# One recurrence unit moved from TensorE transposes to the DMA crossbar, two running sums to a subtraction, one set of decays to small transfers, and all orders written anew

## The chip, the cores and the metric

The kernel runs on one core of one Trainium2 chip. The metric is device time of one execution in microseconds (us); where several executions were timed, their median counts. A core has TensorE (PE, matrix products; its weight loads are listed as PEld), VectorE (DVE), ScalarE (ACT), GpSimd (POOL), and the queue of SyncE (SP), which here only issues DMA transfers. Each engine works its own list of instructions strictly in order and waits on semaphores for the others.

## The reference

Two parts, one behind the other. First a gated linear recurrence for 4 batches of 8 heads over 768 steps with head width 48:

```python
f = 1.0 / (1.0 + np.exp(-f_logit))
for t in range(S):
    state = f[:, :, t, :, None] * state + np.einsum('bhd,bhe->bhde', k[:, :, t], v[:, :, t])
    y[:, :, t] = np.einsum('bhd,bhde->bhe', q[:, :, t], state)
```

Then a gated feed-forward network over the 3072 tokens, with the 8 heads side by side as 384 features and 1536 hidden features:

```python
gate = np.maximum(x @ w_gate, 0.0)
val = x @ w_val
return (gate * val @ w_out)
```

## The kernel before, in words

**Units.** The recurrence is cut into 12 units: `seq` orders them (batch 0 to 3 for the first 256 steps, then for the second, then for the third). A unit is 256 steps of one batch, as two chunks y of 128 steps; a token's even and odd step (index i) lie side by side in one partition of the loaded tile. For each unit `unit(u)` does this:

- Four loads of 384 KB (f, k, q, v) from SP (L449), into four buffers each, so that the load of unit u+4 waits until unit u no longer needs the buffer.
- `exp` and `ln` of the gate on ACT (L536, L538), then running sums along the steps. These are products of TensorE with triangular matrices (L545, L546), two matmuls for the odd steps and, where the unit's setting `even` is `PE`, two more for the even steps. Where `even` is `DVE`, the even ones are the odd ones less one term, a VectorE subtraction in PSUM (L549).
- Exponentials of the sums on ACT (L557, L560, L567) and products with k and q, called hats (L579, L585). With `kps` the exponential for k stays in PSUM and VectorE multiplies; with `qps` the same holds for q.
- k and q must be turned so that features lie in partitions. For units in the set `pe_hats` this is 8 transposes of TensorE for k and 8 for q (L634), each followed by one copy out of PSUM (settings `tk`, `tq`; L647). For the others the hats are written 64 partitions at a time, and two crossbar transposes of the DMA (L655), issued from SP, do it.
- v is copied into a padded tile in pieces of 64 partitions (L619); units in `pe_hats` have two more pieces in another tile (`vrest`, L623).
- Scores of k and q per chunk (L669), masked on VectorE (L683) or copied by ACT and masked on POOL (L678, L680); the state's update (L723 with 8 matmuls of 128 rows, L734 with 16 of 64 rows for `pe_hats`); the output products (L767, L774, L778), whose copies give `xT`, the input of the network, either directly or through one more crossbar transpose (L797).
- The decay of the state over a chunk: a small TensorE sum of 9 matmuls (`total`, L706 and L710) with one ACT exponential (L714), or, where `td` is set and `qps` is not, one store of two rows to DRAM (L690) and four strided loads of them (L699), all from SP.

**The network.** Two units give a group g of 512 tokens. Of its 12 slices of hidden features each takes three matmuls for the gate and three for the value (`ffn_hidden`, L814), ACT's relu (L819) and VectorE's product into `gT` (L821). `ffn_out` takes three matmuls per third of the features and 128 tokens (L837), four such triples give one output tile, which is copied (L851) and stored (L858). Group 0 starts in halves of 256 tokens (r0 and r2) for the first three slices. The weights come in 12 transfers of 288 KB in bf16, four each for `wg`, `wv`, `wo`, three hidden slices each, issued from POOL (L477) because they convert the type.

**Order.** Nothing is ordered by the program text alone: `SEQUENCE` holds, for each engine and for SP, a list of operation numbers written out by hand or by a search, `HOMES` the order in which the tiles of PSUM share the 8 banks, and `FILLERS` a number of matmuls on zeros that TensorE works ahead of a named operation. `Plan.needs` puts the semaphore waits where the order does not already imply them. So an engine with an early wait holds up all that is behind it in its list.

Of the kernel before, what the change touches and what calls it, by code (L numbers as in the profile page):

```python
# [7 lines left out]
F32 = mybir.dt.float32  # L8
BF16 = mybir.dt.bfloat16
# [28 lines left out]
class Plan:  # L38
# [80 lines left out]
    def needs(self, warm):  # L119
# [69 lines left out]
    "ACT": [  # L189
# [9 lines left out]
    "DVE": [  # L199
# [20 lines left out]
}  # L220
HOMES = [
    [
        312, 14, 16, 18, 28, 34, 66, 47, 81, 86, 58, 124, 104, 132, 116, 108, 135, 111, 139, 174, 169, 148, 181, 216, 161, 262, 230, 195, 229, 198,
        232, 211, 236, 269, 251, 246, 258, 288, 297, 301],
    [
        0, 6, 12, 22, 63, 65, 31, 36, 69, 43, 52, 71, 59, 97, 172, 103, 164, 143, 150, 182, 215, 163, 190, 196, 201, 202, 266, 240, 239, 244, 274,
# [23 lines left out]
def bass_hgrn2_outer__then__ffn_reglu_kernel(  # L250
# [14 lines left out]
    HD = H * D  # L265
# [14 lines left out]
    pe_hats = {0, 1, 2, 3, 5}  # L280
# [5 lines left out]
    NU = len(seq)  # L286
# [689 lines left out]
```

## Time and profile before

| what | value |
|---|---|
| median of 3 runs | 194.19 us (193.44 to 194.41) |
| profiled execution | 193.8 us, of which the span from first to last instruction is 192.0 us |
| busy in the span | PE 181.1 us, DVE 126.3, ACT 118.5, POOL 82.8 |
| bytes | 31.89 MB moved, a mean of 166 GB/s |
| granted TensorE clock | 1.00 |

The profile is one execution. A row of a timeline gives the start, the time to the end of the last instruction of the row, engine, line, operation, tiles, form, count, and in brackets the idle time ahead of it with what ended it. Ends of matmuls are modelled, so they overlap; the pace of TensorE is read from one start to the next. In the rows of transfers the last number is the time from issue to landing.

### The profile page before, as it was taken

What the parts mean: (1) busy time and instruction counts of PE and PEld (TensorE: products, weight loads), DVE (VectorE), ACT (ScalarE), POOL (GpSimd) and SP (SyncE); (2) the same over time, 40 slices, a digit from 0 to 9 for tenths busy, and PEclk for the clock granted to TensorE, in tenths of its full rate; (3) what the DMA queues carried; (4) which work ended last, traced back from release to release, by engine and by line L of the source; (5) the groups of instructions that cost most, each with busy time, mean ns of one, the idle gap of its engine ahead of it and who ended that gap; (6) DMA issues with size and microseconds to landing.
All of it is one profiled execution on the core that took longest, in us unless ns stands there. A gap on an engine that the chain in (4) does not pass through costs nothing.

```text
span 192.0 us, 4436 instructions
## 1 busy us (share of the span) xinstructions
PE 181.1 (94%) x1746; PEld 101.0 (53%) x1770; DVE 126.3 (66%) x238; ACT 118.5 (62%) x233; POOL 82.8 (43%) x110
## 2 busy tenths in 40 slices
PE   3998799998999999999999999999999999999994
PEld 1365474545654646455655456454655554445563
DVE  4189864879499999987669989445277452242451
ACT  4998668681997877978687857247702642433511
POOL 4458553994247256754696749007500320000000
DMA  6999999999599999999974792564144050000325
GB/s 156 324 325 285 205 253 206 242 231 199 145 310 220 229 323 255 245 213 189 259 202 79 153 232 59 120 130 123 50 107 79 0 164 3 20 0 0 81 66 164
DMA packets 79088, 31.89 MB, mean 166 GB/s; under 512 B 71254, under 2 KB 79068, under 8 KB 79068
## 3 DMA queue, kind: packets, MB, share of 16 engines
q1 hardware_dynamic: 74268, 28.08, 59.7%
q0 software_dynamic: 4800, 3.54, 11.9%
q8 instruction: 14, 0.23, 0.5%
q14 instruction: 6, 0.05, 0.1%
HBM read 25.96 MB, written 4.73 MB: 160 GB/s over the span
## 4 chain that ended last, share of the span: by engine, by line
PE 75%; DMA 6%; DVE 6%; ACT 4%; SPq 3%; issue 3%; POOL 2%; POOLq 0%
PE ps L814 43%; PE ps L837 22%; DMA wv<-in_moe_w_val_dram 4%; SPq L449 3%; DMA v_in<-in_v_dram 3%; PE ps L669 2%; PE ps L767 2%; DVE gT L821 2%; DVE ptm L683 1%; PE ps L634 1%; ACT ptm L678 1%; ACT relu L819 1%; PE ps L545 1%; DVE vpad L380 1%; POOL vpad L383 1%
## 5 line engine op out<-in xcount | busy, mean ns | idle before, releaser
L821 DVE TENSOR_TENSOR gT<-relu,ps 128x512 bf16<-128x512 bf16 (+1 forms) x75 | 47.7, 660 | 32.9 <-PE ps L814 19.6
L819 ACT ACTIVATE relu<-ps 128x512 bf16<-128x512 f32 (+1 forms) x75 | 41.8, 582 | 37.1 <-PE ps L814 29.1
L837 PE MATMUL ps<-wo,gT 128*128 128x384 bf16 (+2 forms) x300 | 56.2, 320 | 0.9 <-DVE vrest L380 0.8
L814 PE MATMUL ps<-xT,wv 128*128 128x512 bf16 (+1 forms) x214 | 54.6, 370 | 1.3 <-DMA wv<-in_moe_w_val_dram 0.4
L814 PE MATMUL ps<-xT,wg 128*128 128x512 bf16 (+1 forms) x214 | 54.2, 370 | 1.2 <-DMA wg<-in_moe_w_gate_dram 0.5
L680 POOL TENSOR_TENSOR ptm<-ptm,seen 128x512 bf16<-128x512 bf16 x21 | 24.0, 1155 | 39.9 <-ACT ptm L678 39.8
L837 PEld LDWEIGHTS ps<-wo,gT 128*128 128x128 bf16 x300 | 28.0, 98 | 22.4 <-DVE vrest L380 1.2
L814 PEld LDWEIGHTS ps<-xT,wg 128*128 128x128 bf16 x225 | 21.1, 98 | 21.3 <-DMA wg<-in_moe_w_gate_dram 0.8
L814 PEld LDWEIGHTS ps<-xT,wv 128*128 128x128 bf16 x225 | 20.9, 98 | 20.5 <-DVE hats L579 0.6
L683 DVE TENSOR_TENSOR ptm<-ps,seen 128x512 bf16<-128x512 f32 x27 | 18.1, 685 | 1.9 <-PE ps L669 1.7
L585 DVE TENSOR_TENSOR hats<-k_in,ps 64x384 bf16<-64x384 f32 x28 | 15.4, 550 | 5.2 <-ACT ps L567 4.7
L515 POOL TENSOR_TENSOR st<-ssum,dec 128x384 bf16<-128x384 f32 x16 | 13.3, 832 | 11.0 <-DVE ssum L512 10.1
L585 POOL TENSOR_TENSOR hats<-q_in,expo 64x384 bf16<-64x384 f32 x16 | 15.9, 995 | 4.8 <-ACT expo L560 3.8
L678 ACT ACTIVATE ptm<-ps 128x512 bf16<-128x512 f32 x21 | 11.8, 595 | 8.5 <-PE ps L669 8.5
L579 POOL TENSOR_TENSOR hats<-q_in,expo 128x384 bf16<-128x384 f32 x11 | 10.9, 999 | 12.8 <-ACT expo L560 8.2
L382 ACT ACTIVATE osb<-ps 128x384 f32<-128x384 f32 x13 | 6.5, 499 | 12.0 <-PE ps L837 12.0
L560 ACT ACTIVATE expo<-ps 128x384 f32<-128x384 f32 x20 | 9.4, 492 | 3.4 <-DVE ps L549 2.8
L512 DVE TENSOR_TENSOR ssum<-ps,st 128x384 f32<-128x384 f32 x16 | 8.8, 553 | 3.7 <-PE ps L723 2.3
L536 ACT ACTIVATE f_in<-f_in 128x768 f32<-128x768 f32 x12 | 10.2, 847 | 1.1 <-DMA f_in<-in_f_logit_dram 1.0
L567 ACT ACTIVATE ps<-ps 128x384 f32<-128x384 f32 x22 | 10.6, 497 | 0.0
L538 ACT ACTIVATE bneg<-f_in 128x768 bf16<-128x768 f32 x12 | 10.2, 848 | 0.2
L383 DVE COPY osb<-ps 128x384 f32<-128x384 f32 (+2 forms) x12 | 6.2, 520 | 5.5 <-PE ps L837 5.5
(86 smaller groups left out, 185.1 us busy)
## 6 DMA issues: line engine op xcount, KB each, us to landing
f_in<-in_f_logit_dram SPq DMA_DIRECT2D x12, 384.0 KB, 5.8
v_in<-in_v_dram SPq DMA_DIRECT2D x12, 384.0 KB, 5.3
q_in<-in_q_dram SPq DMA_DIRECT2D x12, 384.0 KB, 4.9
k_in<-in_k_dram SPq DMA_DIRECT2D x12, 384.0 KB, 5.4
out_dram<-osb SPq DMA_DIRECT2D x15, 192.0 KB, 2.1
out_dram<-osb SPq DMA_DIRECT2D x16, 96.0 KB, 2.2
wg<-in_moe_w_gate_dram POOLq DMA_DIRECT2D x4, 288.0 KB, 8.4
wv<-in_moe_w_val_dram POOLq DMA_DIRECT2D x4, 288.0 KB, 8.1
```

The source lines that it names most:

```text
L515: add(e, lambda: engine[e].tensor_tensor(t4(s_new), t4(tmp), rate, ALU.mult), [key] + dk, [f"S{b}_{y}"], **(dict(occ=0.79, lat=0.1) if e = ...
L536: add("ACT", lambda cut=cut: sc.activation(raw["f"][:, cut], raw["f"][:, cut], AF.Exp, scale=-1.0), [f"f{li}"], [f"f{li}"], **act_t(2 * HD ...
L567: add("ACT", lambda i=i, ex=ex: sc.activation(bc[i].ap[:, 0:HD] if in_place else ex[:, 1, :], bc[i].ap[:, 0:HD], AF.Exp, scale=1.0), [bc[i ...
L579: add(e, lambda i=i, n=n, x=x, e=e, exps=exps: engine[e].tensor_tensor(hats[:, hi, i, x, :, 0:D], by_i[n][:, i, :, :], exps(), ALU.mult), ...
L585: op = add(e, lambda i=i, n=n, x=x, e=e, y=y, lo=lo, exps=exps: engine[e].tensor_tensor(hats[64 * i:64 * i + 64, hi, y, x, :, 0:D], by_i[n ...
L678: add("ACT", lambda pt=pt, s=sj[j]: sc.activation(pt, s.ap[:, :].rearrange("p (n t) -> p n t", n=NP), AF.Copy), [sj[j]], [f"raw{mis[y]}_{j ...
L680: add("POOL", lambda pt=pt, mask=mask: gp.tensor_tensor(pt, pt, mask, ALU.mult), [f"raw{mis[y]}_{j}", "seen"], [f"raw{mis[y]}_{j}", f"ptm{ ...
L683: add("DVE", lambda pt=pt, mask=mask, s=sj[j]: ve.tensor_tensor(pt, s.ap[:, :].rearrange("p (n t) -> p n t", n=NP), mask, ALU.mult), [sj[j ...
L814: mm = te.matmul(bank.ap[:, 0:n], wt[:, kt, j * 128:(j + 1) * 128], xT[xi][:, kt, n0:n1], start=(kt == 0), stop=(kt == NK - 1))
L819: add("ACT", lambda: sc.activation(relu[ri][:, 0:n], gate.ap[:, 0:n], AF.Relu), [gate], [f"relu{ri}"], **act_t(n))
L821: add("DVE", lambda: ve.tensor_tensor(gT[gi][:, j, n0:n1], relu[ri][:, 0:n], val.ap[:, 0:n], ALU.mult), [val, f"relu{ri}"], [f"gT{gi}_{j}_ ...
L837: mm = te.matmul(bank.ap[:, 0:cut[1] - cut[0]], gT[gi][:, j, r * C:(r + 1) * C], wo[:, j, cut[0]:cut[1]], start=(j == 0), stop=(j == NJ - 1))
```

## The change

Unit 5 leaves `pe_hats`, so its k and q go through the crossbar: 16 TensorE transposes, two copies of PSUM, and two `vrest` pieces go; two DMA transposes on SP come, its hats are four pieces of 64 partitions on VectorE (k) and four on POOL (q), and its state update is the form of L723. Units 6 and 7 take their even running sums by the subtraction. Unit 6 gives up `qps`, its q hats move from VectorE to POOL, and its decays go by one store and four loads on SP in place of `total`. Many settings that name the engine of a copy change, and all five lists, the banks and the fillers are other ones.

```diff
-FILLERS = {66: 4, 84: 11, 89: 2, 232: 5, 124: 1, 127: 2, 153: 1}
+FILLERS = {67: 11, 84: 9, 105: 1, 94: 1, 86: 1, 98: 2, 127: 2, 149: 1}
...
-    pe_hats = {0, 1, 2, 3, 5}
+    pe_hats = {0, 1, 2, 3}
...
```

The settings are one long dictionary per line of code, so only the entries of units 4 to 7 that change are set out here:

```diff
 4
-'v00': 'ACT', 'v10': 'DVE1', 'v11': 'DVE1', 'x0': 'DVE', 'x1': 'DVE', 'o0': 'DVE', 'o1': 'ACT'
+'v00': 'POOL', 'v10': 'ACT', 'v11': 'POOL', 'x0': 'ACT', 'x1': 'ACT', 'o0': 'ACT', 'o1': 'DVE'
 5
-'v00': 'DVE1', 'v01': 'ACT', 'v10': 'ACT', 'x0': 'DVE'
+'v00': 'POOL', 'v01': 'POOL', 'v10': 'DVE1', 'x0': 'ACT', 'x1': 'DVE'
 6
-'even': 'PE', 'qps': True, 'q0': 'DVE', 'q1': 'DVE', 'v01': 'DVE1', 'v10': 'DVE1'
+'even': 'DVE', 'qps': False, 'td': True, 'q0': 'POOL', 'q1': 'POOL', 'v01': 'POOL', 'v10': 'ACT', 'x0': 'DVE', 'x1': 'ACT'
 7
-'even': 'PE', 'v01': 'POOL', 'v11': 'DVE1', 'x0': 'ACT', 'x1': 'DVE', 'o0': 'DVE'
+'even': 'DVE', 'v01': 'DVE1', 'v11': 'ACT', 'x0': 'DVE', 'x1': 'ACT', 'o0': 'ACT'
...
```

Of the lists, three stretches matter below; the numbers are written out as what they name. On POOL, from the first weight on ("mask" is L680, "q hat" L579, "state" L515, "v" L619):

```diff
-wg0, q hat u1, wv0, wg1, wv1, mask u1, wv2, wg2, wg3, wv3, wo0, mask u2, 2 q hats u3, wo1, state u0, wo2, mask u2, wo3
+wg0, q hat u1, wv0, wg1, v u1, wv1, mask u1, wg2, wv2, wv3, mask u2, state u0, wg3, mask u2, q hat u3, wo0, q hat u3, wo1, wo3, wo2
```

On SP, from the first load of unit 4 to the crossbar of unit 6 (a number behind f, k, q, v is the unit):

```diff
-f4 f5 k4 v4 f6, xT u3, q4 v5 v6 k5 q5 f7 f8, crossbar u4, k6, out, q6 f9 f10 q7, out, k7 v7 v8 q8 k8, rates u7, v9, crossbar u6
+v4 f4, xT u3, f5 k4 q4 k5 f6 v5 q5 v6 f7, crossbar u4, k6 q6, crossbar u5, out, k7 f8 v8 f9 q7 v7, rates u6, f10 q8, rates u7, crossbar u6
```

On PE, around the first values of group 0:

```diff
-gate j2, transposes q u2, gates j0 j1, value j1, output products u1, value j0, transposes k u2, value j2
+transposes q u2, gate j1, scores u1, output product u1, gates j2 j0, output product u1, transposes k u2, values j0 j2
```

More of the change, by code (lines that the diff above doesn't have):

```diff
@@ L222 @@
     [
-        312, 14, 16, 18, 28, 34, 66, 47, 81, 86, 58, 124, 104, 132, 116, 108, 135, 111, 139, 174, 169, 148, 181, 216, 161, 262, 230, 195, 229, 198,
-        232, 211, 236, 269, 251, 246, 258, 288, 297, 301],
-    [
-        0, 6, 12, 22, 63, 65, 31, 36, 69, 43, 52, 71, 59, 97, 172, 103, 164, 143, 150, 182, 215, 163, 190, 196, 201, 202, 266, 240, 239, 244, 274,
-        257, 277, 286, 291, 295, 305, 311],
-    [
-        1, 7, 4, 23, 35, 42, 44, 46, 55, 84, 113, 119, 92, 96, 101, 105, 128, 121, 167, 144, 141, 171, 151, 175, 155, 225, 188, 220, 193, 228, 205,
-        264, 213, 209, 242, 248, 256, 259, 253, 293, 294, 308],
@@ L231 @@
-    [
-        3, 9, 5, 11, 19, 25, 33, 68, 48, 79, 53, 72, 74, 90, 91, 98, 95, 114, 106, 134, 178, 146, 140, 147, 184, 154, 159, 261, 200, 207, 263, 233,
-        234, 243, 247, 273, 260, 296, 284, 289, 302, 310],
-    [
-        8, 70, 15, 17, 30, 27, 41, 38, 45, 80, 57, 88, 94, 93, 100, 115, 130, 127, 122, 177, 145, 179, 157, 186, 156, 189, 199, 223, 208, 212, 271,
-        250, 245, 272, 285, 298, 307],
-    [
-        21, 10, 62, 20, 26, 24, 32, 37, 39, 78, 54, 56, 73, 89, 131, 102, 129, 109, 138, 149, 176, 185, 162, 191, 217, 226, 203, 267, 214, 235, 254,
-        281, 280, 306],
@@ L240 @@
-    [
-        13, 60, 29, 67, 75, 49, 50, 83, 87, 118, 123, 125, 133, 166, 107, 110, 137, 173, 170, 152, 158, 224, 192, 218, 197, 222, 204, 265, 238, 268,
-        241, 249, 255, 278, 282, 287, 292, 303, 299, 309],
-    [
-        2, 61, 64, 40, 76, 77, 82, 51, 85, 112, 120, 99, 126, 117, 165, 136, 142, 168, 183, 180, 153, 160, 221, 187, 219, 194, 227, 231, 206, 210,
-        270, 237, 275, 276, 252, 279, 283, 290, 300, 304],
+        307, 7, 21, 22, 17, 64, 40, 76, 54, 86, 51, 113, 123, 97, 117, 104, 125, 109, 110, 143, 149, 175, 171, 156, 257, 216, 189, 223, 202, 197, 200,
@@ new lines @@
+        265, 244, 240, 252, 248, 281, 282, 300, 301, 303],
+    [
+        1, 10, 18, 26, 35, 29, 48, 39, 47, 79, 59, 91, 98, 101, 105, 163, 142, 140, 137, 152, 157, 185, 161, 186, 194, 188, 195, 230, 264, 268, 271,
+        290, 298],
+    [
+        0, 9, 60, 30, 32, 66, 36, 45, 81, 55, 84, 87, 112, 96, 120, 127, 103, 132, 173, 169, 177, 211, 153, 154, 191, 215, 190, 198, 259, 207, 209,
+        245, 232, 270, 241, 243, 272, 274, 279, 277, 286, 285, 304],
+    [
+        3, 8, 12, 16, 20, 70, 25, 24, 33, 67, 38, 49, 44, 52, 71, 58, 88, 89, 119, 115, 102, 126, 121, 136, 144, 148, 146, 176, 210, 184, 213, 222,
+        201, 227, 206, 266, 242, 254, 250, 283, 280, 289, 305],
@@ new lines @@
+    [
+        2, 4, 61, 31, 41, 46, 42, 82, 56, 124, 95, 131, 122, 133, 134, 168, 167, 179, 151, 220, 159, 183, 199, 218, 226, 260, 237, 267, 273, 278, 297,
+        296, 293, 306],
+    [
+        14, 15, 19, 65, 34, 69, 43, 57, 99, 116, 130, 108, 107, 172, 164, 145, 147, 170, 180, 181, 182, 187, 214, 221, 196, 205, 228, 246, 269, 253,
+        276, 275, 288, 294],
+    [
+        13, 62, 11, 28, 27, 68, 83, 37, 78, 80, 50, 72, 73, 118, 93, 114, 128, 162, 135, 165, 178, 150, 219, 225, 192, 224, 203, 258, 208, 233, 229,
+        236, 234, 239, 249, 255, 291, 292, 284, 302],
@@ L246 @@
+    [
+        6, 5, 63, 23, 75, 77, 53, 85, 74, 90, 92, 129, 94, 100, 106, 111, 141, 139, 166, 138, 174, 158, 155, 160, 256, 212, 193, 217, 204, 261, 262,
+        263, 235, 238, 231, 247, 251, 287, 295, 299],
 ]
-FILLERS = {66: 4, 84: 11, 89: 2, 232: 5, 124: 1, 127: 2, 153: 1}
+FILLERS = {67: 11, 84: 9, 105: 1, 94: 1, 86: 1, 98: 2, 127: 2, 149: 1}
 def bass_hgrn2_outer__then__ffn_reglu_kernel(
```

16 lines of the change are left out of this document (8 added, 8 removed), and 80 rows, old and new, of the table SEQUENCE.

## The prediction

> **What bounds the kernel now.** I read the page's busy times first, then a table by stage, then TensorE's timeline for the places where it really stops.
>
> ```profile
> PE 181.1 (94%) x1746; PEld 101.0 (53%) x1770; DVE 126.3 (66%) x238; ACT 118.5 (62%) x233; POOL 82.8 (43%) x110
> ```
>
> ```profile
> 0.00:24.00 24.00, 18.02 (x232) 9.98 (x238) 16.21 (x44) 18.35 (x35) 13.63 (x34) 1.00 1.09 259
> 24.00:48.00 24.00, 22.90 (x248) 13.65 (x250) 17.38 (x33) 15.26 (x32) 15.64 (x20) 1.00 1.18 226
> 48.00:76.00 28.00, 27.55 (x388) 15.97 (x391) 24.54 (x45) 23.34 (x47) 12.77 (x15) 1.00 0.99 246
> 76.00:98.00 22.00, 21.68 (x235) 12.04 (x238) 16.43 (x29) 18.40 (x36) 14.69 (x17) 1.00 0.97 231
> 98.00:190.00 92.00, 90.94 (x655) 49.37 (x664) 51.77 (x89) 43.15 (x86) 26.04 (x27) 1.00 0.37 86
> ```
>
> The columns of the table are the stretch, then busy time and count of PE, PEld, DVE, ACT, POOL, then clock, DMA share and GB/s. From 24 us on PE is busy 163.07 of 166 us, at full clock; DVE is nearly as full only from 48 to 76 us, and the DMA engines are full until 98 us. So the end is set by when the first weights land and by how much PE work follows. Where does PE stop after that? Once for long:
>
> ```profile
> 44.15 1.62 PE L837 MATMUL ps<-wo,gT 128*128 128x384 bf16 x9
> 46.61 0.65 PE L837 MATMUL ps<-wo,gT 128*128 128x384 bf16 x3 [0.84 <-DVE vrest L380]
> 47.10 0.36 PE L778 MATMUL ps<-vpad,ptm 128*128 128x48 bf16 x8
> 38.38 0.80 POOL L477 DMA_DIRECT2D wo<-in_moe_w_out_dram  x1
> ...
> wo<-in_moe_w_out_dram POOLq DMA_DIRECT2D x1, 288.0 KB, 8.1
> ```
>
> An output triple goes from start to start in 47.10 - 46.61 = 0.49, so nine matmuls take 1.47 and PE stood from 45.62 to 46.61, 0.99 us. The row names a DVE copy, but the fourth `wo` transfer was issued at 38.38 and landed 8.1 later, at 46.48. The triple that starts at 46.61 is the first that needs it. I read this as a wait for weights. The head shows the same: gate and value products begin as their first weights land.
>
> ```profile
> 14.24 0.93 POOL L477 DMA_DIRECT2D wg<-in_moe_w_gate_dram  x1 [1.07 <-DMA k_in<-in_k_dram]
> 21.52 0.50 PE L814 MATMUL ps<-xT,wg 128*128 128x256 bf16 x3 [0.47 <-DMA wg<-in_moe_w_gate_dram]
> 23.49 0.49 PE L814 MATMUL ps<-xT,wv 128*128 128x256 bf16 x3 [0.37 <-DMA wv<-in_moe_w_val_dram]
> ...
> 21.45 1.15 POOL L680 TENSOR_TENSOR ptm<-ptm,seen 128x512 bf16<-128x512 bf16 x1 [2.85 <-ACT ptm L678]
> 22.56 0.80 POOL L477 DMA_DIRECT2D wv<-in_moe_w_val_dram  x1
> ...
> wv<-in_moe_w_val_dram POOLq DMA_DIRECT2D x1, 288.0 KB, 7.5
> wg<-in_moe_w_gate_dram POOLq DMA_DIRECT2D x1, 288.0 KB, 8.9
> ```
>
> The last two rows are the transfers issued at 22.56 and, behind it, 23.36: they landed at 30.1 and 32.3, so one behind another costs 2.2 us, and none landed in under 7.2.
>
> **The change part by part.** What leaves PE is priced from the chain of waits (start, time, what) and the timeline:
>
> ```profile
> 47.46 0.45 PE ps L734 x16
> 57.09 0.34 PE ps L723 x8
> 64.77 0.45 PE ps L634 x8
> 65.87 0.45 PE ps L634 x8
> ```
>
> ```profile
> 30.32 0.33 PE L545 MATMUL ps<-bneg,upto 128*128 128x384 bf16 x1
> 30.48 0.33 PE L546 MATMUL ps<-bneg,upto 128*128 128x384 bf16 x1
> 30.64 0.81 PE L814 MATMUL ps<-xT,wg 128*128 128x512 bf16 x3
> 31.29 1.46 PE L814 MATMUL ps<-xT,wv 128*128 128x512 bf16 x6
> ...
> 43.92 0.17 PE L706 MATMUL ps<-away,other 128*128 128x16 bf16 x1
> 43.95 0.34 PE L710 MATMUL ps<-halves,bneg 128*128 128x4 bf16 x8
> ```
>
> Unit 5: 16 transposes, 2 x 0.45 = 0.90; its state update 0.45 - 0.34 = 0.11. Units 6 and 7: one pair of running-sum matmuls each, 30.32 to 30.64, 2 x 0.32 = 0.64. Unit 6: `total`, 43.92 to 44.15, 0.23. Sum 1.88 us, all behind 41 us where PE has no slack. First term: -1.88. The two fillers more lie ahead of the first weights, where PE waits anyway: nothing.
>
> What the other engines get, by groups of equal shape (count, busy, mean ns):
>
> ```profile
> L585 POOL TENSOR_TENSOR hats<-q_in,expo 64x384 bf16<-64x384 f32 x16 | 15.9, 995 | 4.8 <-ACT expo L560 3.8
> L585 DVE TENSOR_TENSOR hats<-k_in,ps 64x384 bf16<-64x384 f32 x28 | 15.4, 550 | 5.2 <-ACT ps L567 4.7
> L549 DVE TENSOR_TENSOR ps<-ps,bneg 128x384 f32<-128x384 f32 x7 | 3.9, 563 | 2.7 <-PE ps L546 2.6
> L579 DVE TENSOR_TENSOR hats<-q_in,ps 128x384 bf16<-128x384 f32 x4 | 2.2, 546 | 0.0
> L383 DVE COPY qkT<-ps 128x1024 bf16<-128x1024 bf16 x6 | 4.1, 689 | 2.5 <-PE ps L634 2.5
> ```
>
> DVE: unit 5's k hats become four pieces for two whole ones of about the same 0.55, +1.10; two subtractions, +1.13; a PSUM copy goes, -0.69; two `vrest` pieces of 64 partitions at about 0.55, -1.10; unit 6's two q hats, -1.09. That is -0.65, and copies of units 4 and 5 move off it besides: I cost DVE at nothing. POOL gets two more pieces for unit 5 (+2.0) and unit 6's q hats (+2.0) where it worked 12.77 of 28 us and 14.69 of 22: covered by its idle time, unless a piece is late for the crossbar. ACT loses a copy. If DVE's cover is gone, its stage of 48 to 76 us is what would end late, since the network's next group waits for its `xT`.
>
> **The head.** `wg0` still waits for k1, which is ninth on SP in both lists, so PE's first gate stays near 21.5. Behind it the new list puts a POOL mask and a state product of other units ahead of `wg3`, and a mask and a q hat more ahead of `wo0`. By the orders, unit 2's scores come near 27.1 instead of 29.1 (four network products worth 1.63 moved behind them, the rest from work drawn ahead of the first value); ACT's copy, POOL's mask (1.15) and state follow, and `wg3` goes out near 30.4, `wo0` near 34.3 (ACT's three score copies set the second mask). For their landing I take 7.3, the transfer that like these had none in front of it:
>
> ```profile
> wo<-in_moe_w_out_dram POOLq DMA_DIRECT2D x1, 288.0 KB, 7.3
> ```
>
> That is `wg3` at 37.7 and `wo0` at 41.6. Before, the first gate of the last slice ran at 37.36 and the first output triple at 40.61; in the new list the triple has one hidden product (31.29 - 30.64 = 0.65) less and one `total` (0.23) more behind it. So PE is late by 41.6 - 40.6 + 0.65 - 0.23 = +1.4 there. The bounds: 0 if POOL gets there as early as before, +3 if each slice takes the 8.9 of the queued one. Then the 0.99 of the last `wo` goes: the last two are issued near 37 and are wanted near 48.6. Third term -1.0.
>
> The Trainium skill, page "DMA: Bandwidth & Descriptors", section "Anatomy of one DMA", fits a GpSimd transfer as about 2.0 us plus its bytes over 436 GB/s, an estimate of 2.7 us for 288 KB; the 7.2 to 8.9 here are against it, and the measurement decides. By the page `wg3` would land at 33.1 and the +1.4 would vanish.
>
> **SP and the crossbars.** Two transposes and five small transfers come into SP between 58 and 96 us.
>
> ```profile
> 53.71 1.15 SPq L449 DMA_DIRECT2D q_in<-in_q_dram  x1
> 54.90 3.25 SPq L449 DMA_DIRECT2D f_in<-in_f_logit_dram  x2
> 58.25 4.53 SPq L655 DMA_TRANSPOSE qkT<-hats  x2
> ...
> qkT<-hats SPq DMA_TRANSPOSE x14, 3.2
> ...
> dec<-rates SPq DMA_DIRECT2D x12, 0.8 KB, 2.4
> ```
>
> The first rows follow each other without a gap: SP is full there. In the new list the xT transpose of unit 3 goes earlier: its product follows the first output triple (41.6), so SP is through with it near 44.2; nine loads of 1.2 follow, unit 4's crossbar from 55 (4.5 for its two), k6 and q6, then unit 5's, issued near 61.2 and, half of 4.53 later, 63.5. The second lands 3.2 later, near 66.8. On PE, 9 triples, 2 hidden products and 2.2 us of recurrence lie between 41.6 and unit 4's sums, so these come at 49.5; 7 triples, 19 hidden products and 2.3 us of recurrence later, near 67.6, unit 5's scores are due. That is 0.8 us of slack, and unit 6's crossbar, by the same count, has 0.3 (81.5 against 81.8). A wait there is +0.4, from 0 (both in time) to +3 (SP's loads slow, rival 2). Behind SP's waits stand the loads of units 7 to 10, wanted later. Unit 6's decays (five issues, 2.4 to land) are wanted only near 88: nothing.
>
> On "X-Bar Transpose (TRN2)" the Trainium skill's page "Advanced Engine Details and Errata" says that transposes are as fast as plain transfers. SP's 4.53 for two of 128 KB, against 3.25 for two loads of 384 KB, does not bear it out. By the page the pair would take an estimated third of the loads' 3.25, unit 5 would have over 3 us of slack, and the sum would be 0.4 lower.
>
> Sum: -1.88 + 1.4 - 1.0 + 0.4 = -1.1. Against the profiled execution's own 193.8 (span 192.0 and 1.8 around it) that is 192.7. The profiled run is 0.4 under the median of 194.19, so against the median it would be 193.1; I keep 192.7.
>
> **The rivals.** (1) The weights come in time: POOL's list has the early masks done sooner, the +1.4 shrinks to 0.2 and no crossbar waits: -1.88 - 1.0 + 0.2 = -2.7, 191.1. For it speaks that POOL waited 2.85 us for one mask, a wait that can shrink. Against it, two late issues, not one. (2) Slower: unit 5's crossbar is late. Its place is PE's scores of unit 5; everything of group 2 hangs on them. If the nine loads ahead of it on SP take 1.6 each (3.25 / 2) instead of the 1.15 of the row ahead, it lands 4 later, 3.2 past its slack: -1.5 + 3.2 = +1.7, 195.5. It decides from about 2.9 us of wait on. For it: SP is full there. Against: the nine loads include those that ran late before, and the weights are through by 48. (3) The change does not do what it says: PE's freed work turns into many small waits, because the old lists leave PE almost none and new ones, with DVE at 24.54 of 28, rarely fit as well. Price: the 1.1 is lost, 193.8 to 194.5.
>
> **How the numbers follow.** Half a percent, about what a measurement of this kernel can tell from no change, is 0.97 us: faster is under 193.2, slower over 195.2. Forecast (192.0 to 193.4) 0.38; rival 1 0.17; rival 2 0.20; rival 3 0.25. Faster: 0.33 of the forecast and rival 1, 0.50. Slower: rival 2 and 0.02 of rival 3, 0.22. The rest, 0.28, is the same. The range leaves out rival 2's upper part and the lowest of rival 1: 191.0 to 195.4.
>
> **What would show it.** PE's matmuls down by 37 beside the fillers, no L634 near 65; a gap of PE ahead of a `wg` product near 37 and ahead of the first `wo` triple near 41, none at 46; gaps ahead of unit 5's scores under 1 us. The prediction is wrong if the first gate moves from 21.5, if PE stands over 2 us before unit 5's or 6's scores, or if PE has many gaps of 0.3 us behind 98 us, where it had none.

## The result and the profile after the change

The changed kernel takes 192.45 us (median of 20 runs, 191.4 to 194.34) where the kernel before took 193.9 beside it (20 runs, 193.4 to 195.32). The ratio is 0.9926, 95% interval 0.9907 to 0.9945: 1.4 us, 0.7 %, faster. Measured again later, unedited, beside other kernels of the study it took 191.65 against 193.5 of the kernel before, ratio 0.9917 (0.9894 to 0.9939). The forecast was 192.7, within 192.0 to 193.4. The sum came out; two of its terms did not, and this is what the rest is about.

The profiled execution of the changed kernel took 192.23 us, its span is 190.5, 1.5 under the span before. The busy times, and the table by stage with the columns of the prediction's:

```profile
PE 182.6 (96%) x1735; PEld 99.3 (52%) x1735; DVE 128.5 (67%) x240; ACT 111.7 (59%) x217; POOL 91.9 (48%) x125
```

```profile
0.00:24.00 24.00, 19.29 (x265) 10.37 (x269) 16.51 (x44) 16.55 (x32) 15.96 (x38) 1.00 1.09 259
24.00:48.00 24.00, 23.73 (x285) 14.14 (x280) 18.87 (x37) 17.11 (x34) 14.56 (x17) 1.00 1.16 225
48.00:76.00 28.00, 28.00 (x325) 15.01 (x313) 23.64 (x42) 22.73 (x45) 20.11 (x26) 1.00 1.09 258
76.00:98.00 22.00, 21.99 (x237) 11.61 (x235) 17.81 (x32) 16.66 (x31) 14.27 (x16) 1.00 0.94 220
98.00:188.40 90.40, 89.62 (x655) 48.18 (x653) 51.65 (x89) 38.64 (x77) 27.05 (x30) 1.00 0.44 92
```

TensorE is full from 24 us on, and POOL's work of 48 to 76 us grew from 12.77 to 20.11 without TensorE noticing. One caution: the matmul counts before (1746) and after (1735) differ by 11, not by 35, because the trace of before lacks 24 matmul records (its weight loads, which are all there, count 1770, those of after 1735). So the busy time of PE can't be compared; start times of the same instruction can, and all that follows uses those.

Where TensorE waited, by the view that groups its waits; first before, then after, lines that belong to the network and to the recurrence behind 20 us:

```profile
PE ps L837 <- DVE vrest L380: 0.8, 1, 0.8
...
PE ps L814 <- DMA wg<-in_moe_w_gate_dram: 0.5, 1, 0.5
```

```profile
PE ps L814 <- DMA wg<-in_moe_w_gate_dram: 0.7, 1, 0.7
```

The wait of 0.8 ahead of an output triple is gone, as forecast. What came in its place is small and stands in the timeline of the changed kernel (matmuls, and weight loads where they carry the wait):

```profile
37.60 1.46 PE L814 MATMUL ps<-xT,wg 128*128 128x512 bf16 x6
...
40.85 0.65 PE L837 MATMUL ps<-wo,gT 128*128 128x384 bf16 x3
...
44.59 0.09 PEld L734 LDWEIGHTS ps<-vpad,hats 64*128 64x128 bf16 x1 [0.52 <-ACT vpad L382]
...
45.18 0.09 PEld L734 LDWEIGHTS ps<-vpad,hats 64*128 64x128 bf16 x1 [0.22 <-DVE gT L821]
...
67.55 0.45 PE L669 MATMUL ps<-qkT 48*128 48x128 bf16 x10
...
80.34 0.24 PEld L723 LDWEIGHTS ps<-vpad,hats 128*128 128x128 bf16 x5 [0.50 <-ACT vpad L382]
```

```profile
78.91 0.84 ACT L536 ACTIVATE f_in<-f_in 128x768 f32<-128x768 f32 x1 [0.46 <-DMA f_in<-in_f_logit_dram]
```

The last gate slice's product at 37.60, the first output triple at 40.85 and unit 5's scores at 67.55 have no wait. The state updates of unit 2 (44.59), unit 3 (45.18) and unit 6 (80.34) have one. A weight load can run ahead of its matmul, so its idle time overstates the loss; start to start, the matmul stream stood 0.31, 0.23 and 0.35 there, 0.89 in all. The one at 80.34 starts at a load: unit 6's value copy stands in ACT's list behind unit 10's exponential, the last row, for whose `f` ACT waited 0.46 us (it landed at 78.89). The copy ran from 79.77 to 80.29.

Behind the last matmul: the last PSUM copy and the last store, before and after.

```profile
189.67 0.29 DVE L383 COPY osb<-ps 128x128 f32<-128x128 f32 x1 [0.24 <-PE ps L837]
...
189.99 0.34 SPq L858 DMA_DIRECT2D out_dram<-osb  x1
```

```profile
187.66 0.29 DVE L383 COPY osb<-ps 128x128 f32<-128x128 f32 x1 [0.25 <-PE ps L837]
...
188.34 0.45 SPq L858 DMA_DIRECT2D out_dram<-osb  x1
```

The copy ends 2.01 earlier, but the store is issued 0.03 behind it before and 0.39 after, since SP is still busy with the stores ahead of it; from the copy's end to the end of the span it is 2.04 before (192.0 - 189.96) and 2.55 after.

So the 1.5 of the profile adds up: first output triple +0.24 (40.61 to 40.85), of which 0.23 is unit 3's `total` that now stands ahead of it; from there to the last matmul -2.24 (148.80 to 146.56), which is -1.88 of removed work, -0.23 for that same `total`, -0.99 for the wait that went and +0.89 for the three new ones; tail +0.5.

### The profile page after: what moved, and what is told of

It reads as the page before. It is cut to its first block, busy times and chain, and to the rows that moved or that the text cites. A ratio compares the mean times of both kernels' runs of the same rounds, so it can differ in the third digit from the quotient of the medians.

```text
span 190.5 us, 4402 instructions
## 1 busy us (share of the span) xinstructions
PE 182.6 (96%) x1735; PEld 99.3 (52%) x1735; DVE 128.5 (67%) x240; ACT 111.7 (59%) x217; POOL 91.9 (48%) x125
## 4 chain that ended last, share of the span: by engine, by line
PE 83%; DMA 6%; DVE 4%; SPq 2%; issue 1%; POOL 1%; POOLq 0%
PE ps L814 48%; PE ps L837 24%; DMA wg<-in_moe_w_gate_dram 4%; PE ps L669 3%; PE ps L767 3%; DMA v_in<-in_v_dram 3%; SPq L449 2%; DVE ptm L683 1%; PE ps L723 1%; DVE gT L821 1%; PE ps L545 1%; POOL vpad L383 1%; PE ps L634 1%; PE ps L546 1%; PE ps L778 1%
## 5 line engine op out<-in xcount | busy, mean ns | idle before, releaser
L821 DVE TENSOR_TENSOR gT<-relu,ps 128x512 bf16<-128x512 bf16 (+1 forms) x75 | 48.0, 661 | 32.6 <-ACT relu L819 19.4
L814 PE MATMUL ps<-xT,wg 128*128 128x512 bf16 (+1 forms) x225 | 56.1, 371 | 0.7 <-DMA wg<-in_moe_w_gate_dram 0.7
L814 PE MATMUL ps<-xT,wv 128*128 128x512 bf16 (+1 forms) x225 | 55.5, 371 | 0.0
L837 PE MATMUL ps<-wo,gT 128*128 128x384 bf16 (+2 forms) x300 | 55.1, 320 | 0.0
L680 POOL TENSOR_TENSOR ptm<-ptm,seen 128x512 bf16<-128x512 bf16 x21 | 24.0, 1152 | 39.8 <-ACT ptm L678 37.5
L814 PEld LDWEIGHTS ps<-xT,wg 128*128 128x128 bf16 x225 | 20.6, 98 | 20.9 <-DMA wg<-in_moe_w_gate_dram 1.0
L585 POOL TENSOR_TENSOR hats<-q_in,expo 64x384 bf16<-64x384 f32 x20 | 19.9, 994 | 4.6 <-ACT expo L560 2.0
L585 DVE TENSOR_TENSOR hats<-k_in,ps 64x384 bf16<-64x384 f32 x32 | 17.5, 551 | 3.5 <-ACT ps L567 2.8
L579 POOL TENSOR_TENSOR hats<-q_in,expo 128x384 bf16<-128x384 f32 x10 | 10.4, 1040 | 8.6 <-ACT expo L560 8.4
L515 POOL TENSOR_TENSOR st<-ssum,dec 128x384 bf16<-128x384 f32 x16 | 13.1, 827 | 2.9 <-DVE ssum L512 1.7
L560 ACT ACTIVATE expo<-ps 128x384 f32<-128x384 f32 x22 | 10.1, 490 | 6.7 <-DVE ps L549 4.8
L383 POOL CAST vpad<-v_in 64x384 bf16<-64x384 f32 x23 | 11.5, 501 | 4.0 <-DMA v_in<-in_v_dram 2.8
L382 ACT ACTIVATE osb<-ps 128x384 f32<-128x384 f32 x12 | 5.7, 492 | 11.1 <-PE ps L837 11.1
## 6 DMA issues: line engine op xcount, KB each, us to landing
out_dram<-osb SPq DMA_DIRECT2D x15, 192.0 KB, 2.2
```

Of the source, the lines that this page charges most:

```text
L383: return engine[e].tensor_copy(out, src)
L515: add(e, lambda: engine[e].tensor_tensor(t4(s_new), t4(tmp), rate, ALU.mult), [key] + dk, [f"S{b}_{y}"], **(dict(occ=0.79, lat=0.1) if e = ...
L579: add(e, lambda i=i, n=n, x=x, e=e, exps=exps: engine[e].tensor_tensor(hats[:, hi, i, x, :, 0:D], by_i[n][:, i, :, :], exps(), ALU.mult), ...
L585: op = add(e, lambda i=i, n=n, x=x, e=e, y=y, lo=lo, exps=exps: engine[e].tensor_tensor(hats[64 * i:64 * i + 64, hi, y, x, :, 0:D], by_i[n ...
L680: add("POOL", lambda pt=pt, mask=mask: gp.tensor_tensor(pt, pt, mask, ALU.mult), [f"raw{mis[y]}_{j}", "seen"], [f"raw{mis[y]}_{j}", f"ptm{ ...
L814: mm = te.matmul(bank.ap[:, 0:n], wt[:, kt, j * 128:(j + 1) * 128], xT[xi][:, kt, n0:n1], start=(kt == 0), stop=(kt == NK - 1))
```

## The experiments

The times are medians. Each kernel ran beside the kernel before on the same chip, so ratios are to that, and the changed kernel's own is 0.9926. "Standing" is time between two matmul starts beyond what the first one takes.

### The freed matmuls put back: sums of units 6 to 11

```diff
-  units 6 to 11: 'even': 'DVE'
+  units 6 to 11: 'even': 'PE'
```

> The changed kernel with one part undone and widened: the running sums of units 6 to 11 (not 6 and 7 alone) are made by a second pair of matmuls again in place of a DVE subtraction. Theory (TensorE has no slack behind 41 us, so its work is the time): six pairs of 0.32 us, 1.9 us more than the changed kernel's 192.45, 194.4, that is about 0.5 us above the kernel before, with no new wait in TensorE's timeline. Rival (the freed matmuls were not what paid, DVE's subtractions cost as much as they free): six subtractions of 0.56 leave DVE as well, and the time stays within 0.6 of 192.45.

Measured: 193.88, ratio 1.001 (0.9983 to 1.0038); 1.001 - 0.9926 is 1.6 us more than the changed kernel. The timeline shows unit 6's second pair back:

```profile
68.73 0.33 PE L545 MATMUL ps<-bneg,upto 128*128 128x384 bf16 x1
68.89 0.33 PE L546 MATMUL ps<-bneg,below 128*128 128x384 bf16 x1
69.05 0.33 PE L545 MATMUL ps<-bneg,upto 128*128 128x384 bf16 x1
69.22 0.33 PE L546 MATMUL ps<-bneg,upto 128*128 128x384 bf16 x1
```

Set against the changed kernel instruction by instruction, this stream falls back by about 0.3 at each of the six places, 1.9 in all, and wins 0.34 back at 80 us, where unit 6's state update now comes late enough to find its value copy ready. From 45.2 us, where the two are level, to the end the net is 1.5. So TensorE's work is the time, at full price behind 81 us, and the two pairs that the change removed in front of that (0.64) brought only 0.30: the rest went into the wait at 80. DVE lost six subtractions of 0.56 and nothing was won by that, so in the changed kernel DVE costs nothing.

### Unit 5 back on TensorE

```diff
-  pe_hats = {0, 1, 2, 3}
+  pe_hats = {0, 1, 2, 3, 5}
   PE:   state update of unit 4; 16 transposes of unit 5's k and q; ...
-  SP:   two crossbar transposes of unit 5
```

> The changed kernel with the first part of the change undone: unit 5's q and k are transposed by 16 TensorE transposes again (whole hats, two copies from PSUM, two vrest pieces), right behind unit 4's state update; SP has no crossbar for unit 5. Theory (the crossbar took 0.90 of transposes and 0.11 of state update off the path and cost no wait): 1.0 us more than the changed kernel, 193.3 to 193.6. Rival (what the crossbar saves it costs again as waits, or copies on DVE and ACT cost beside): outside of that, under 192.7 or over 194.

Measured: 192.72, ratio 0.9952 (0.9925 to 0.9979), 0.5 us more than the changed kernel: under the theory's 193.3 and at the edge of the rival's 192.7, with an interval of the difference as wide as the difference. The profiles say more than the times:

```profile
61.44 1.06 PE L633 MATMUL ps<-ident,hats 128*128 128x128 bf16 x16
```

Against the changed kernel the stream falls back 0.89 at the transposes and 0.20 at unit 5's state update, 1.09 for the 1.01 that I had priced, and again wins 0.34 at 80 us: 0.75. The price was right, the yield was not: in these profiles a third of what unit 5's crossbar saved on TensorE (0.34 of 1.09) was lost to the same value copy, and so to the load ahead of it.

### Unit 5's crossbar later

```diff
   SP:  loads k, q of unit 6
-       crossbar of unit 5, both halves
        store of row 0, load k of unit 7, load f of unit 8
+       crossbar of unit 5, both halves
```

> The changed kernel with unit 5's two crossbar transposes put behind three more entries of SP's list (one output store, two loads: 0.58, 0.44 and 0.68 us of issue by its trace). In the changed kernel the second lands at 67.16 and the scores that need it start at 67.55, 0.39 us of slack. Theory (rival 2's mechanism exists, only not its size): landing near 68.9, a gap of 1.3 us ahead of unit 5's scores, and the time 1.3 more, 193.7. Rival (what follows has room to take it up): a gap, but under 0.5 us at the end, 192.4 to 192.9.

Measured: 195.78, ratio 1.0074 (1.0041 to 1.0108), 2.9 us more than the changed kernel. The timeline, SP and TensorE:

```profile
61.69 1.79 SPq L858 DMA_DIRECT2D out_dram<-osb  x1
...
64.93 3.98 SPq L655 DMA_TRANSPOSE qkT<-hats  x2
...
70.88 0.51 PE L669 MATMUL ps<-qkT 48*128 48x128 bf16 x12 [2.51 <-DMA qkT<-hats]
```

The mechanism holds, and of the loss only the 0.35 at 80 us comes back behind it; the size was missed twofold, for the store alone took 1.79 of SP instead of 0.58. In this profile the first gate came 0.54 later and 0.7 was lost at the first output triple too, so not all of the 3.3 by which its span is longer is the crossbar's: 2.57 arises at unit 5's scores. Nor is all of the 2.9 in the medians: in six of its twelve executions the mean granted clock was 0.989 to 0.991 and the time 196.00 to 197.19, in the other six 0.998 to 1.000 and 194.04 to 195.55, with a median of 194.5, 2.0 above the changed kernel. About 1 of the 2.9 goes with the clock. The second rival of the prediction was a real mechanism with a real price; in the changed kernel it is 0.39 us away (landing 67.16, scores 67.55).

### SP's loads ahead of the transpose it stands at

```diff
   SP:  loads v, f of unit 4
-       xT of unit 3
        loads f5, k4, q4, k5, f6
+       xT of unit 3
```

(The expectation misnames one slot: the five are f5, k4, q4, k5 and f6.)

> The changed kernel with SP's order near 33 us changed: the transpose of unit 3's xT, behind which SP stood from 33.6 to 42.25 us, goes behind five loads (f, k and q of unit 5, k of unit 4, f of unit 6 by their slots). Theory A (the late weights landed in 5.2 to 5.8 us and not in the 7.3 that I took because SP stood and no load was in flight beside them): with loads beside them wg3 takes 7 or more and lands near 38, wo0 near 42, TensorE shows gaps ahead of the last gate product (37.60 before) and ahead of the first output triple (40.85 before), 1 to 1.4 us together, and the time is 193.5 to 193.9, unless the earlier loads save as much later, which the trace of the changed kernel gives no place for. Theory B (a weight transfer's time hangs on what is queued ahead of it on POOL alone): wg3 and wo0 land as before, no gap, 192.2 to 192.6.

Measured: 195.97, ratio 1.0089 (1.0056 to 1.0122). Neither theory gave that. SP in the changed kernel, then in this one:

```profile
42.25 1.28 SPq L797 DMA_TRANSPOSE xT<-xn  x1
43.58 0.58 SPq L449 DMA_DIRECT2D f_in<-in_f_logit_dram  x1
```

```profile
36.51 1.20 SPq L449 DMA_DIRECT2D k_in<-in_k_dram  x1
37.76 2.58 SPq L449 DMA_DIRECT2D q_in<-in_q_dram  x1
40.43 3.78 SPq L449 DMA_DIRECT2D k_in<-in_k_dram  x1
44.31 3.59 SPq L449 DMA_DIRECT2D f_in<-in_f_logit_dram  x1
47.95 1.84 SPq L797 DMA_TRANSPOSE xT<-xn  x1
```

With weights and loads together in flight a load takes up to 3.8 us of SP, where the first ones behind xT took 0.6 in the changed kernel, and xT, ready near 42, goes out at 47.95. TensorE stood for that, not for weights:

```profile
52.24 0.81 PE L814 MATMUL ps<-xT,wg 128*128 128x512 bf16 x3 [2.45 <-DMA xT<-xn]
```

For the weights theory A holds in part. wg3 and wo0 landed as before (6.0 and 5.7 behind their issue, against 5.8 and 5.6), but the last three slices took 6.9, 8.3 and 9.7 where they took 5.2, 5.9 and 6.6. The group of the last two, here and in the changed kernel, with the median of its landings at the end of the line:

```profile
wo<-in_moe_w_out_dram POOLq DMA_DIRECT2D x2, 288.0 KB, 9.0
```

```profile
wo<-in_moe_w_out_dram POOLq DMA_DIRECT2D x2, 288.0 KB, 6.2
```

### In the kernel before: the last weights issued earlier

```diff
   POOL: wo1
-        state product of unit 0
-        wo2
-        mask of unit 2
-        wo3
+        wo2
+        wo3
+        state product of unit 0
+        mask of unit 2
```

> The kernel before with its last two wo transfers issued right behind the second one (a state product and a mask go behind them): 35.6 and 36.4 in place of 36.45 and 38.38. Theory (the 0.99 us that TensorE stood from 45.62 to 46.61 was a wait for the fourth wo transfer, though the row named a DVE copy): it lands near 45, the gap goes, 192.9 to 193.1 against 193.9. Rival (the copy of vrest by DVE was the wait): the gap stays, 193.6 to 194.1, or grows by the mask that is later.

Measured: 193.78, ratio 1.0007 (0.9984 to 1.003): no change. The triple that had waited for a "DVE vrest":

```profile
46.37 0.48 PE L837 MATMUL ps<-wo,gT 128*128 128x384 bf16 x2 [0.61 <-DMA wo<-in_moe_w_out_dram]
```

Now the row names the transfer. It was issued 1.98 us earlier, at 36.40, and landed at 46.23 instead of 46.48; the triple moved by the same 0.24, from 46.61 to 46.37. So the wait was for the transfer, and what sets its landing is not its issue: it took 9.8 instead of 8.1. The last three weights landed 2.1 and 2.25 us apart in both orders of the kernel before (42.11, 44.23, 46.48, and here 41.98, 44.09, 46.23), and 1.4 to 1.5 apart in the changed kernel (41.68, 43.10, 44.58). So an earlier issue only waits longer behind the transfers ahead of it; what differs in the changed kernel is the pace.

### In the kernel before: SP stands, as it does after

```diff
   SP:  loads f of units 4 and 5
-       loads k4, v4, f6
-       xT of unit 3
+       xT of unit 3
+       loads k4, v4, f6
```

> The kernel before with one entry of SP's list moved: the transpose of unit 3's xT goes ahead of three loads (k and v of unit 4, f of unit 6; issued at 35.05, 38.74 and 41.95 before), so that SP stands there while the last three output slices are under way, as it does in the changed kernel. Theory (the wait at 45.6 is for the fourth wo transfer, and that is late because loads are in flight beside it, not because of its issue): the fourth wo lands at 45 or sooner instead of 46.48, TensorE's gap of 0.99 goes, and the three loads are 5 us or more later; if unit 4's and unit 5's hats have that room, the time is 192.7 to 193.0 against 193.6 to 193.9. Rival (the room is not there): the gap goes and comes back ahead of unit 4's sums or scores, 193.5 or more.

Measured: 195.36, ratio 1.0113 (1.0078 to 1.0148). The rival. The same triple, and what comes behind it:

```profile
45.57 0.32 PE L837 MATMUL ps<-wo,gT 128*128 128x384 bf16 x1
```

```profile
56.27 0.10 PEld L545 LDWEIGHTS ps<-bneg,upto 128*128 128x128 bf16 x1 [0.86 <-ACT bneg L538]
...
57.82 0.37 PEld L723 LDWEIGHTS ps<-vpad,hats 128*128 128x128 bf16 x8 [0.84 <-DVE hats L585]
```

```profile
54.58 0.84 ACT L536 ACTIVATE f_in<-f_in 128x768 f32<-128x768 f32 x1 [1.69 <-DMA f_in<-in_f_logit_dram]
```

The fourth `wo`, issued at 38.06, took 7.4 and landed at 45.43, with one load left beside it (landed at 44.16). The triple came 1.04 sooner, without a wait. Then what the loads that were held back to 48.55 feed was late: ACT stood 1.69 us for an `f` issued at 49.79 and landed at 54.55, the last row, and TensorE stood 1.8 us between 54 and 58. This pair of runs explains the 0.99: it is what the loads on SP take from the weights on POOL, it can be had by holding the loads, and in the old order holding them costs more. The new order holds nine loads for 8.6 us and has the room.

### wo0 issued earlier

```diff
   POOL: wg3
+        wo0
         mask of unit 2, q hat of unit 3
-        wo0
```

> The changed kernel with one transfer moved: the first output slice, wo0, is issued right behind wg3 (near 31.5 us) and no longer behind a mask and a q hat (34.68), in a stretch where POOL stood 1.1 us for its next mask. In the profile of the changed kernel wo0 took 5.6 and landed at 40.25, ahead of its triple; in three executions with the same head it took 6.7 to 7.0 and TensorE stood 0.67 to 0.79 there. Theory (the late issue of wo0 costs 0 to 0.8, by what SP's loads have in flight, and the median holds about half of it): wo0 lands before 39.5, no gap ahead of the first output triple, 191.9 to 192.2. Rival 1: wg3, now with company, is late for its gate at 37.6, 192.5 or more. Rival 2: the time won is given back at the next wait (state update of unit 2 at 44.6, scores of unit 5), 192.3 to 192.6.

Measured: 192.51, ratio 0.9929 (0.9905 to 0.9954): no change. wo0 was issued at 31.77 and landed at 39.17, 1.9 ahead of its triple, which had no wait; but so it had in the first profile of the changed kernel. Others with the same head had one; two of them:

```profile
41.27 0.65 PE L837 MATMUL ps<-wo,gT 128*128 128x384 bf16 x3 [0.63 <-DMA wo<-in_moe_w_out_dram]
```

```profile
42.05 0.65 PE L837 MATMUL ps<-wo,gT 128*128 128x384 bf16 x3 [0.50 <-DMA wo<-in_moe_w_out_dram]
```

They are of the runs with the sums put back and with the later crossbar. In each of them wo0 took 6.7 or more, and the loads ahead of it had begun near 24 instead of 21.8 us, so that the last of them landed at 41.3 and 41.7, 7.2 and 6.4 behind wo0's issue (38.75, 4.1 behind it, in the first profile). So the wait at the first triple comes and goes with SP's loads, 0 or about 0.7. Where it came, 0.45 of it was won back at 44.6 and 45.2, where TensorE would have stood anyway. So taking it out can gain 0.25 at most, less than these runs can tell (the interval of the ratio is 0.9 us wide). The time alone fits both rivals of the expectation; the one that holds up `wg3` is out by the trace, in which it landed at 36.69 with no wait at its gate.

### The first gate slice earlier

```diff
-  wg0@k1
+  wg0@q1
```

> The changed kernel with one edit: the first gate slice's transfer no longer waits for the load of k of unit 1 (1.07 us of POOL's idle time ahead of the issue at 14.31) but for the load of q of unit 1, two loads earlier. Theory (the end is set by when the first weights land and by how much TensorE work follows): wg0 lands about 1.0 us earlier, the gap of 0.83 us ahead of the first gate product goes, the time falls by up to 0.8, 191.6. Rival (the DMA engines are full there, so what the weights gain the loads of units 1 and 2 lose): wg0 lands as before, or unit 1's scores are late by as much; 192.2 to 193.

Measured: 192.68, ratio 0.9943 (0.992 to 0.9966): no gain. The first gate, the first triple and unit 5's scores:

```profile
20.85 0.38 PE L814 MATMUL ps<-xT,wg 128*128 128x256 bf16 x2
...
40.80 0.65 PE L837 MATMUL ps<-wo,gT 128*128 128x384 bf16 x3 [0.59 <-DMA wo<-in_moe_w_out_dram]
...
67.65 0.46 PE L669 MATMUL ps<-qkT 48*128 48x128 bf16 x10 [0.53 <-DVE gT L821]
```

The gate came 0.80 earlier, and the triple only 0.05, because wo0 took 6.8. The 0.45 of waits at 44.6 and 45.2 came back too, and at unit 5's scores (67.65 against 67.55) nothing is left: the second half of their crossbar landed at 67.56, whatever the row names. Behind that, unit 6's state update came at 81.00 instead of 80.34, after ACT had waited 1.01 us for unit 10's `f`. So a head start of TensorE alone was worth nothing: wo0, unit 5's crossbar and that load didn't come earlier with it.

### Small waits taken out by moving TensorE's work

```diff
   POOL: wo0 behind wg3
   PE:  +one output triple ahead of unit 2's state update, one more ahead of unit 3's
   PE:  +one hidden product ahead of unit 7's state update
   SP:  +first half of unit 5's crossbar ahead of loads k6, q6
-  SP:  both stores of row 20
+  ACT: both stores of row 20
```

> The changed kernel with the small waits that its trace shows taken out by order alone: wo0 behind wg3; unit 2's state update one output triple later and unit 3's two (TensorE stood 0.31 and 0.23 ahead of them at 44.1 and 44.9); unit 7's state update one hidden product later (0.35 at 80); the first half of unit 5's crossbar ahead of two loads; and the two stores of row 20 issued by ACT's queue, since SP's last stores follow back to back and the last one is issued 0.39 behind its copy. Theory (these waits are what kept the change from its sum): 0.5 + 0.35 + 0.4 and up to 0.7 of wo0 less, 190.6 to 191.3. Rival (TensorE's waits are tied to transfers, and what is won ahead is given back at the next one): 191.8 to 192.5.

Measured: 193.65, ratio 0.9995 (0.9971 to 1.0018): 1.3 worse than the changed kernel. That is above the forecast and above the rival's range too. Three of the edits were mistakes, and the trace names them:

```profile
46.14 0.66 PE L837 MATMUL ps<-wo,gT 128*128 128x384 bf16 x3 [0.66 <-DVE st L508]
...
185.76 2.69 ACTq L859 DMA_DIRECT2D out_dram<-osb  x2
...
188.57 0.49 ACT L382 ACTIVATE osb<-ps 128x384 f32<-128x384 f32 x1 [2.84 <-PE ps L837]
```

The triple that went behind unit 2's state update takes the PSUM bank which that update fills, and waits until DVE has read it: 0.82 standing for 0.54 saved. The state update at 80 us is unit 6's, and I moved unit 7's. And ACT's two store issues took 2.69, so that its copy of row 22 began 0.14 behind the start of the last matmul (188.43), where in the changed kernel it began 1.40 ahead of it; the end lies 3.7 behind the start of the last matmul instead of 3.1.

### Small waits taken out where they come from, and wg0 with them

```diff
   POOL: wo0 behind wg3
   ACT: +unit 2's two value copies ahead of unit 3's first score copy
   ACT: +unit 6's value copy ahead of unit 10's exponential
   SP:  +both halves of unit 5's crossbar ahead of loads k6, q6
   (second kernel)  wg0@k1 -> wg0@q1
```

The changed kernel ran beside both, unedited.

> The changed kernel itself, unedited, beside the next two on the same chip: 192.2 to 192.7. In its first profile TensorE did not stand ahead of the first output triple; in three profiles with the same head it stood there 0.67 to 0.79. If that wait comes and goes with SP's loads, this profile shows either 0 or about 0.7, and with it a landing of wo0 5.6 or 6.7 and more behind its issue.

> The changed kernel with its small waits taken out where they come from, and not by moving TensorE's work: ACT makes unit 2's two value copies ahead of unit 3's first score copy, where it stood 1.01 us, and unit 6's value copy ahead of unit 10's exponential; wo0 goes out behind wg3; both halves of unit 5's crossbar go out right behind unit 4's, ahead of two loads. Theory (the 0.54 at 44 to 45 us and the 0.35 at 80 are waits for these ACT copies, and unit 5's scores follow at once because a crossbar that follows a crossbar takes 1.3 of SP and lands near 65.6): 0.9 less than the changed kernel on the same chip, 191.4 to 191.8. Rival (a wait that is taken out comes back at the next transfer): 192.2 to 192.6.

> The same as the one before, and the first gate slice's transfer waits for the load of q of unit 1 instead of k of unit 1, as in the run that brought the first gate 0.80 earlier and lost it again at the first output triple. Theory (there it was lost to wo0, to ACT's copies and to unit 5's crossbar, all of which are out of the way here): up to 0.8 less than the one before, 190.7 to 191.2. Rival (transfers of the early weights and the loads share the DMA engines, so that another of them is late): the same as the one before, or slower.

Measured on one chip, against 193.5 of the kernel before: the changed kernel 191.65, ratio 0.9917 (0.9894 to 0.9939); with the waits taken out 191.73, 0.9914 (0.9899 to 0.9928); with wg0 earlier as well 191.21, 0.988 (0.9866 to 0.9895).

The changed kernel's triple had no wait here, and wo0 took 5.7: the no-wait side of the expectation, but its 191.65 lies 0.6 below the range given for it. The 0.35 at 80 us was gone in this profile without any edit: unit 10's `f` had landed at 76.92, and ACT did not wait for it. Taking the waits out alone gains nothing against the changed kernel beside it, where 0.9 was forecast; its 191.73 fits the forecast only because that kernel itself came out lower. The wait at 80 us goes, and of the 0.54 nothing is won in the end: unit 2's update comes 0.22 sooner, so ACT's copy had held it, but unit 3's update, right behind it, waits for DVE's product `gT`, which ends at 45.11 where it ended at 45.12. Its row is now:

```profile
45.17 0.09 PEld L734 LDWEIGHTS ps<-vpad,hats 64*128 64x128 bf16 x1 [0.42 <-DVE gT L821]
```

What is won at one wait comes back at the next. With wg0 earlier on top, what was lost in the run with wg0 alone stays won:

```profile
20.72 0.27 PE L814 MATMUL ps<-xT,wg 128*128 128x256 bf16 x1
...
40.06 0.33 PE L837 MATMUL ps<-wo,gT 128*128 128x384 bf16 x1
```

Against the first profile of the changed kernel the gate comes 0.93 sooner, the first triple 0.79, unit 5's scores 0.78 (66.77, with the crossbar landed at 64.77), the last matmul 0.74. ACT's wait for unit 10's `f` is there again (0.61 us) and costs nothing now, since unit 6's copy stands ahead of it. This version takes 1.2 % less than the kernel before and 0.5 us less than the version without the wg0 edit, where the intervals don't meet. Against the changed kernel it is 0.4 us by the medians and 0.7 by the ratios, and the two intervals just touch, so that part is likely but not shown.

## Why the prediction came out, step by step

**TensorE is the bound (right).** The sums put back cost their full price behind 81 us, and 0.3 less in total for the part of it in front of 80 us.

**-1.88 of removed work (right as work, 0.34 too much as time).** Unit 5's part was priced 1.01 and measured 1.09. What I did not see is that TensorE, earlier by that much, reaches unit 6's state update ahead of ACT's value copy, which stands behind an exponential that waits for a load. In the first profile that load was late, in the second it was not and the wait was gone, so the 0.34 is not lost in every execution. I had asked what a step removes, and not, for each removed piece, which operand of the next instructions would now come last.

**DVE and POOL cost nothing (right).** No wait behind 48 us names a DVE hat or a POOL piece, and removing six subtractions bought nothing.

**The head, +1.4 (wrong: 0.0 in the first profile, up to about 0.7 in others).** Two things failed. The 7.3 for a transfer with none in front of it: wg3 took 5.8 and wo0 5.6, so they landed at 36.50 and 40.25, ahead of 37.60 and 40.85, though both were issued where I had put them (30.72 and 34.68, forecast 30.4 and 34.3). And the hidden product worth 0.65: counted again from the two orders, 16 full and 12 half products stand ahead of the first triple in both; only the `total` moved. Without the 0.65 the term would have been about 0.8, which is what the profiles show in which wo0 took 6.7 to 7.0 and the triple waited; the wait at `wg3` that I also expected came in neither profile of the changed kernel. The Trainium skill's fit (page "DMA: Bandwidth & Descriptors", section "Anatomy of one DMA"), an estimate of 2.7 us, was further off: no weight transfer in these profiles took under 5.2.

**-1.0 for the fourth `wo` (right in place and size, wrong in its reason).** I let it go because the issue comes earlier. The issue came at 38.03, 0.35 earlier. It landed 1.90 earlier, because SP stood from 33.6 to 42.25 with nine loads behind xT. Issuing it 2 us earlier in the old order moved its landing by 0.25.

**Crossbars, +0.4 (wrong by size: 0).** Unit 5's was issued at 60.99 and 63.98 (forecast 61.2 and 63.5) and landed at 67.16 (66.8), with 0.39 of slack where I had 0.8; unit 6's at 81.96 with 0.8 where I had 0.3. The Trainium skill's rule that crossbar transposes are as fast as plain transfers is not borne out: 54.69 and 60.99 below each stand for two transposes. Each moves 256 KB (128 x 1024 in bf16), not the 128 KB of the prediction. Two thirds of a plain load of 384 KB each, by that rule and the prediction's 3.25 for the pair of loads, is an estimate of 2.2 us for the two; they took 4.90 and 4.30 behind loads and 2.57 behind another transpose, so the rule is off by less than the prediction's numbers make it.

**What the sum lacked.** The two terms that fell short, 1.4 and 0.4, were mostly made up by 0.89 of new waits and 0.5 in the tail, neither of which I had. Rival 3 (freed work turns into small waits) had the right mechanism for half of it. So that the total came out is luck: its wrong terms cancel. In the second profile of the changed kernel, where the wait at 80 didn't show and the end lay 2.7 behind the last matmul's start instead of 3.1, the span is 189.5, and the 191.65 of that measurement lies under the range.

## What to carry to other kernels

When loads and weights share the DMA engines, ask when a transfer lands by what is in flight beside it, not by when it is issued: a reordered load queue moved the weights by 2 us, and an earlier issue by 0.25. Time freed on the bounding engine is worth its full price only as far as the operands of the next instructions are early: count the slack of each of them, 0.39 us here, before adding gains up. And a gain at the start holds only if each later meeting point with another queue is moved too: wg0 alone gained nothing, with three others moved it gained about 0.5.

## What the runs showed of the hardware

**What a DMA issue costs its queue depends on what stands right ahead of it.** SP in the changed kernel:

```profile
54.69 4.90 SPq L655 DMA_TRANSPOSE qkT<-hats  x2
...
60.99 4.30 SPq L655 DMA_TRANSPOSE qkT<-hats  x2
```

Of each pair, the first, behind loads, took 3.55 and 2.94, the second, behind a transpose, 1.31 both times; where unit 5's pair was put right behind unit 4's, its two took 1.23 and 1.34. The dear ones follow the loads with no more than 0.15 us between them: where SP had stood 0.81 or 3.10 us behind its loads, in the run with the loads ahead of xT, the first of a pair took 1.63 and 1.24. In the changed kernel a load takes 0.4 to 5.1 us of SP and a store 0.3 to 1.6, in the kernel before up to 6.9 and 2.1; two stores took 2.69 of ACT.

**Loads and weights share.** The Trainium skill, page "DMA: Bandwidth & Descriptors", section "SWDGE vs HWDGE vs iDMA", says that transfers issued by GpSimd and those issued by SP enter different queues inside each DMA engine, which takes from them in turn. The traces agree as far as they go: the last `wo` took 8.1 to 9.8 where SP went on loading beside it (three kernels) and 6.6 to 8.0 where SP stood, with one exception, 9.6 in the last version, where a load issued at 32.6 landed only at 45.2.

**One gap halved the clock, another of the same length did not.** With the loads ahead of xT, TensorE stood from 49.5 to 52.2 us. The table by windows (clock in the third column from the end):

```profile
53.00:54.00 1.00, 1.00 (x7) 0.49 (x5) 0.00 (x0) 0.92 (x2) 0.92 (x2) 0.69 1.17 326
54.00:56.00 2.00, 2.00 (x8) 0.99 (x7) 0.00 (x0) 1.78 (x3) 1.81 (x4) 0.50 1.16 321
56.00:57.00 1.00, 1.00 (x5) 0.47 (x4) 0.52 (x1) 0.00 (x0) 0.11 (x1) 0.60 1.27 299
57.00:58.00 1.00, 1.00 (x16) 0.68 (x14) 0.82 (x3) 0.00 (x0) 0.00 (x0) 1.00 0.78 155
```

About a microsecond after work came back the granted clock fell to 0.50, and stayed there for some 3.4 us (0.31 / 0.50 of the first window, all of the second's 2 us, 0.40 / 0.50 of the third). Against the changed kernel that cost another 1.7: a wait of 2.6 cost 4.3. The gap of the same length ahead of unit 5's scores left the clock at 1.00 in the profile of the run with the later crossbar. Six of that kernel's twelve executions, though, had a mean clock of 0.989 to 0.991. Over a span of some 190 us that is as much as 3.4 us at 0.50, so there the gap was probably caught; those executions were not profiled. The changed kernel's executions never fell under 0.997. The Trainium skill, page "TensorE: Matmul & The Clock Gate", section "Part 1: The HAM clock gate (the "warmup" mystery)", says that a window of about 3.4 us, which runs freely, decides on the clock. The length of the slow stretch agrees, and a free-running window would explain why one gap was caught and the other not; that a gap of 2.6 us can be enough is shown here and is less than an idle window.
